# An adaptive-LayerNorm transformer block: gates applied to the results instead of folded into the weights, queries masked by VectorE instead of placed by DMA, blocks in plain order

## The chip, the cores and the metric

The kernel runs on one core of one Trainium2 chip. The metric is the time of one execution on the device in microseconds (us), the median of several runs. A core has five engines that run their own instruction queues in order: TensorE (PE, matrix products into PSUM), VectorE (DVE), ScalarE (ACT), GpSimd (POOL) and SyncE (SP, which here only issues DMAs).

## The reference

Input `x` is 2048 rows of 512 columns, bf16; attention has 32 heads of 16 columns. A conditioning row `c` gives shifts, scales and gates.

```python
mod = (_silu(c) @ w_mod).reshape(c.shape[0], 6, 1, -1)
sa, ca, ga, sb, cb, gb = ...                       # six rows of 512
h = _layernorm(x, axis=-1) * (1 + ca) + sa
x = x + ga * _A_ref(h, A_wqkv, A_wo)               # attention, then @ wo
h = _layernorm(x, axis=-1) * (1 + cb) + sb
x = x + gb * _B_ref(h, B_w1, B_b1, B_w2, B_b2)     # @ w1 + b1, gelu, @ w2 + b2; 1376 hidden columns

# _A_ref
scores = jnp.einsum('bhqd,bhkd->bhqk', q, k) * Dh ** (-0.5)
p = _softmax(scores, axis=-1)
o = jnp.einsum('bhqk,bhkd->bhqd', p, v)
```

32 heads with 2048 x 2048 scores each are 134 million exponentials. They are the largest piece of work in the kernel.

## The kernel before

The program is written by a scheduler inside the kernel: every piece of work is an `op` with an engine, a guessed duration and its dependencies, and the order in which each engine's queue stands is decided while the program is built. On the chip the queues are fixed.

Attention goes in 32 runs. A run takes one block of 512 queries and four heads of one group of eight (`cc` is the group, 0 to 3), against 16 key tiles of 128 keys. For each key tile there are four score matmuls of 128 x 512, one per head. The exponentials of a key tile go one of two ways:

```python
# ACT: two or three score tiles at a time, PSUM -> bf16
nc.scalar.activation(out=e.tile[:, 0:len(got) * QB], in_=o.tile[:, 0:len(got) * QB],
                     func=ACT.Exp, scale=ESC)                                     # L842, pt<-st
# DVE: an exponential out of integer arithmetic: the score as bits of a bf16 ...
nc.vector.tensor_scalar(out=ph.tile[:, ...], in0=o.tile, scalar1=PH_B, scalar2=0.0,
                        op0=ALU.add, op1=ALU.max)                                 # L883, ph<-ax, 4 per key tile
# ... and four shifted copies, whose weighted sum smooths the error
nc.vector.tensor_scalar(out=o.tile, in0=first.tile, scalar1=PH_SH[j], scalar2=None,
                        op0=ALU.add)                                              # L898, sh<-ph, 4 per key tile
```

Four of the 16 key tiles of a run (`DKS = (2, 6, 10, 14)`; one of 16 in the first run) may go to DVE. When ACT has nothing else to do it takes one of these too; the scheduler decides which. Either way the products with the values gather in the PSUM bank `od` (L931). So ACT and DVE share the exponentials, and PE feeds both.

The parts that the change touches:

```python
# queries: one scaled evacuation, then eight DMAs into a tile that is zero elsewhere
# (two tiles side by side, the even and the odd heads)
qs = op("DVE", lambda o: nc.vector.tensor_scalar(
    out=o.tile, in0=mm.tile[:, 0:QB], scalar1=QSC, scalar2=None, op0=ALU.mult), ...)   # L695
def place(o):
    for i in range(8):
        at = slice(16 * i, 16 * i + 16)
        nc.sync.dma_start(out=qm.tile[at, i % 2, :], in_=qs.tile[at, :])               # L702

# order of runs: two blocks of queries with the first group of heads, then the two with the second
early = [(1, 0),(0, 1),(1, 1)]
groups = [(0, 0)] + early + [(b, cc) for b in range(NQ) for cc in range(NC) if ...]

# gates: GpSimd multiplies the weights once, in halves of 256 columns
def scaled(parts, gate_t, deps):
    for w in parts:
        got += beside(lambda c, w=w: nc.gpsimd.tensor_tensor(
            out=w()[:, c], in0=w()[:, c], in1=gate_t[:, c], op=ALU.mult), deps, prio=2.0)
...
# so a residual is one add that reads the product from PSUM, for each 128 rows
nc.vector.tensor_tensor(out=x2.tile[:, t, :], in0=a.tile, in1=xr.tile[:, t, :], op=ALU.add)   # L1137
nc.vector.tensor_tensor(out=o.tile, in0=mm.tile, in1=x2.tile[:, t, :], op=ALU.add)            # L1185
```

The last block of 512 queries is taken in two halves. The first half's projection and MLP are done while the second half's attention runs; of its 11 slices of hidden columns the first `PSUM_F = 4` are evacuated by DVE into `g` (L1164) and get their gelu after the last exponential, and the other seven are multiplied after it and go through gelu straight from PSUM (L1160). Gelu and exponential use different tables of ACT, so gelus of the last block are put after the last exponential. The tail after it then holds the second half's projection, residual, LayerNorm and MLP (L1220 to L1281).

Of the kernel before, what the change touches and what calls it, by code (L numbers as in the profile page):

```python
# [12 lines left out]
ALU = mybir.AluOpType  # L13
# [238 lines left out]
def kernel(  # L252
# [14 lines left out]
    nc = tc.nc  # L267
# [23 lines left out]
    AHEAD = 3  # L291
    PSUM_F = 4
    FIRST_DKS, D_TIME = (14,), 8.0
# [10 lines left out]
    def res(name, n, shape, dt, pool=work):  # L304
        return Res(name, n, lambda i: pool.tile(shape, dt, name=f"{name}{i}"))
# [15 lines left out]
                                   work.tile([P, TPB], FP32, name=f"rs{i}")))  # L321
    QM = [keep.tile([P, 2, QB], BF16, name=f"qm{n}") for n in range(4)]
    r_qm = Res("qm", 4, lambda i: QM[i])
    r_qs = res("qs", 2, [P, QB], BF16)
    r_OD = res("OD", 2, [P, QB], FP32)
    r_RB = res("RB", 1, [P, QB], FP32)
    r_OT = res("OT", 6, [P, QB], BF16)
    r_OS = res("OS", 2, [P, QB], BF16)
    r_o = res("o", 2, [P, D], BF16)
    r_dc = res("dc", 2, [P, 16], FP32)  # L330
# [79 lines left out]
    def dma(fn, deps=(), kb=64, eng="SP", n=1, **k):  # L410
        o = op(eng, fn, 0.45 * n, deps, **k)
        o.kb = kb
        return o
# [270 lines left out]

    o_qz = [op("POOL", lambda o, n=n: nc.gpsimd.memset(QM[n], 0.0), 1.0, prio=0.5 + n) for n in range(1, 4)]

    def make_q(b, cc, kind, acq):
        qm = op("NIL", None, 0.0, (), lat=0.0, prio=0.0, acq=r_qm)
        mm = proj(b, o_w[0], cc, kind, acq, after=qm)
        if (b, cc) == (0, 0):  # L690
            evs = [op("DVE", lambda o, p=p: nc.vector.tensor_scalar(
                out=qm.tile[:, p, :], in0=mm.tile[:, 0:QB], scalar1=qmask[:, p:p + 1], scalar2=None,
                op0=ALU.mult), 0.6, (mm, qm, o_mask), prio=0.1 if p == 0 else 0.45, rel=(mm,)) for p in range(2)]
        else:
            qs = op("DVE", lambda o: nc.vector.tensor_scalar(  # L695
                out=o.tile, in0=mm.tile[:, 0:QB], scalar1=QSC, scalar2=None, op0=ALU.mult), 0.6, (mm, qm),
                prio=0.3, acq=r_qs, rel=(mm,))

            def place(o):
                for i in range(8):  # L700
                    at = slice(16 * i, 16 * i + 16)
                    nc.sync.dma_start(out=qm.tile[at, i % 2, :], in_=qs.tile[at, :])  # L702
            evs = 2 * [dma(place, [qs] + o_qz, kb=128, n=8, prio=0.4, rel=(qs,))]
        o_q[(cc, b)] = (qm, evs)
        qm.uses += 1
        q_left[(cc, b)] = 8 * NT
# [30 lines left out]

    early = [(1, 0),(0, 1),(1, 1)]
    groups = [(0, 0)] + early + [(b, cc) for b in range(NQ) for cc in range(NC) if (b, cc) not in [(0, 0)] + early]
    runs = [(b, 2 * cc + p) for b, cc in groups[:LAST * NC] for p in range(2)] + [(LAST, u) for u in range(8)]  # L740
    wait = {cc: 2 * groups.index((0, cc)) for cc in range(NC)}
    NR = len(runs)
# [259 lines left out]

    def scaled(parts, gate_t, deps):
        got = []
        for w in parts:
            got += beside(lambda c, w=w: nc.gpsimd.tensor_tensor(
                out=w()[:, c], in0=w()[:, c], in1=gate_t[:, c], op=ALU.mult), deps, prio=2.0)
        return op("NIL", None, 0.0, got, lat=0.0, prio=0.0)

    def w2_scaled():  # L1010
        return scaled([lambda f=f: W2[f // 4].tile[:, f % 4, :] if f < 8 else W2c[:, f - 8, :] for f in range(NF)],
                      gb_bc, (W2[0], W2[1], o_late["small"], o_late["gb"]))

    def beside(fn, deps, rel=(), prio=0.5):
# [68 lines left out]


    def wo_mm(ps, b, t, lo, hi):
        for u in range(lo, hi):
            ot, at = (o_OT[(b, (t // 2) * NC + u)], (t % 2) * P) if b == LAST else (o_OT[(b, u)], t * P)
            nc.tensor.matmul(out=ps, lhsT=ot.tile[:, at:at + P], rhs=Wo[:, u, :],
                             start=(u == 0), stop=(u == NC - 1))
# [34 lines left out]
    def block_tail(b, nt=TPB):  # L1124
# [8 lines left out]
        for t in range(nt):  # L1133
            a = chain([(lambda ps, t=t, u=u: wo_mm(ps, b, t, u, u + 1), MM) for u in range(NC)],
                      [x for u in ots for x in u.two] + [prev], kind, r_ax, ots, 2)
            prev = a
            res_done.append(op("DVE", lambda o, t=t, a=a: nc.vector.tensor_tensor(  # L1137
                out=x2.tile[:, t, :], in0=a.tile, in1=xr.tile[:, t, :], op=ALU.add), 0.6,
                (a, xr), prio=0.1, rel=(a,)))
        h, hd, za, trs = layer_norm(lambda t: x2.tile[:, t, :], res_done, modB, o_late["mB"],  # L1140
# [39 lines left out]
        for t in range(nt):  # L1180
            mm = chain([(lambda ps, t=t, f=f: w2_mm(ps, g.tile, t * P, f, f + 1), MM)
                        for f in range(NF)], (prev, one, o_late["w2"]), "part" if part else kind, r_ax, (g,), 3,
                       lambda f: ge[0] if not part else ge[f >= 2] if f < PSUM_F else ev[f])
            prev = mm
            a = op("DVE", lambda o, t=t, mm=mm: nc.vector.tensor_tensor(  # L1185
                out=o.tile, in0=mm.tile, in1=x2.tile[:, t, :], op=ALU.add), 0.6,
                (mm,), prio=3.0 if part else 0.1, acq=r_o, rel=(mm, x2))
            dma(lambda o, t=t, a=a: nc.sync.dma_start(
                out=out[0][b * QB + t * P:b * QB + (t + 1) * P, :], in_=a.tile), (a,), kb=128,
                rel=(a,))  # L1190
# [3 lines left out]
    def last_half():  # L1194
# [17 lines left out]
        for n, t in enumerate(tiles):  # L1212
# [18 lines left out]
            def wo2(o, t=t):  # L1231
                for p in range(2):
# [4 lines left out]
                   ml + [early[t]], lat=PEL, mode=full, kind="last", prio=0.2)  # L1237
            a = op("DVE", lambda o, t=t: nc.vector.tensor_tensor(
                out=x2.tile[:, t, :], in0=acc[t].tile, in1=xr.tile[:, t, :], op=ALU.add), 0.62,
                (w, x2, xr), prio=0.024 + n / 50, rel=(acc[t],))  # L1240
            s = op("DVE", lambda o, t=t: stats(ln, t, x2.tile[:, t, :]), 0.83, (a, ln), prio=0.022 + n / 50)
# [31 lines left out]
            for f in range(NF):  # L1273
# [6 lines left out]
                prev = o  # L1280
            a = op("DVE", lambda o, t=t, first=first: nc.vector.tensor_tensor(  # L1281
                out=o.tile, in0=first.tile, in1=x2.tile[:, t, :], op=ALU.add), 0.66, (prev,), prio=0.1,
                acq=r_o, rel=(first,))
            dma(lambda o, t=t, a=a: nc.sync.dma_start(
# [6 lines left out]
    for b in range(NQ):  # L1291
# [14 lines left out]
        make_v(b, 0, kind, r_ax, "DVE")  # L1306
    o_w[0].uses += 1
    for cc in range(1, NC):
        due(32 + APR * (2 * cc - 1) - CB + (wait[cc] - 2 * cc) * APR * 1, CB * 0.7 / 8 + 0)
        for b in range(NQ):  # L1310
            make_k(b, cc, f"c{cc}", r_ax, "DVE", o_k[(0, min(b + AHEAD, LAST))])
            make_v(b, cc, f"c{cc}", r_ax, "DVE", o_k[(0, min(b + AHEAD, LAST))])
# [9 lines left out]
    def want_q(g):  # L1322
        while q_made[0] < g and q_made[0] + 1 < NQ * NC:
            q_made[0] += 1
            b, cc = groups[q_made[0]]
            due(32 + APR * (first_run(q_made[0]) - 1) - 32)
            make_q(b, cc, f"q{q_made[0]}", r_ax)
            due(1e9)
            if cc == NC - 1:
                o_h[b].uses -= 1  # L1330

    state = {"late": 0}
    qk_a()
    want_q(1)
    while True:
# [7 lines left out]
        while ended:  # L1343
# [4 lines left out]
            for cc in range(1, NC):  # L1348
                if r >= wait[cc] - 3:
                    urgent.add(f"c{cc}")  # L1350
                if r >= 2 * cc - 3:
                    urgent.add(f"in{cc}")
# [4 lines left out]
            if r == 0:  # L1357
                late_loads(o_last[0])
                o_late["ga"] = gate_bc(ga_bc, o_late[2], "gate")
                o_late["wo"] = scaled([lambda u=u: Wo[:, u, :] for u in range(NC)] +  # L1360
                                      [lambda p=p: WoP[:, p, :] for p in range(2)], ga_bc,
                                      (o_late["wo"], o_late["ga"]))
                lt = {3: o_late[3], 4: o_late[4]}
                gt = o_late["g"]

                class V:
                    pass
                va, vb = V(), V()
                o_late["mB"] = None
                state["gt"] = gt  # L1370
# [9 lines left out]
            if r == 6:  # L1380
                for i in range(2):
                    W2[i] = load_w(B_w2[4 * i * P:4 * (i + 1) * P, :].rearrange(
                        "(j p) n -> p j n", p=P), r_w, (), prio=5.0)
                o_late["w2"] = w2_scaled()
                state["w2"] = True
# [38 lines left out]
```

## Time and profile before

| what | value |
|---|---|
| time, median of 3 runs | 797.8 us (797.3 to 799.59) |
| span of the profiled execution | 795.5 us |
| granted TensorE clock, mean | 0.996 |
| exponentials on ACT (L842), 631 instructions | 717.5 us busy |
| `ph` and `sh` on DVE (L883, L898), 472 each | 308.2 and 309.7 us busy |
| residual adds from PSUM (L1137, L1185, L1238, L1281), 32 | 0.68 to 0.69 us each |
| weight multiplications on GpSimd (L1006), 34 | 0.67 to 0.68 us each |
| `qm<-qs` DMAs, 120 of 16 KB | issue 0.58 us each (median) on SP |
| first exponential starts | 16.0 us |
| last exponential ends | 770.6 us |

A line of the groups names the source line, the engine, the operation and `out<-in` by the program's names, with shapes and count; after the bar stand the busy time of the group and the mean nanoseconds of one instruction, then the idle time of the engine just before it and what ended most of that. A line of the waits says who waited for whom: microseconds in total, times, the longest. The chain that ended last goes back from the last instruction to what released it, step by step, and gives the shares of the span by engine.

### The profile page before, as it was taken

Reading aid. Unit: us, or ns where it says so; the run is one execution under the profiler, and the core shown is the slowest. Engines: PE = TensorE matmul, PEld = TensorE weight load, DVE = VectorE, ACT = ScalarE, POOL = GpSimd, SP = SyncE. Lnnn points to the kernel's source line nnn. Section 1 sums busy time; section 2 is a strip of 40 time slices with the busy share of each in tenths; the row PEclk is TensorE's granted clock in tenths of the full one; section 3 lists DMA queues with packets and bytes.
Section 4 is the critical chain, followed back from the end, with each engine's and each line's share of the span. In section 5 each row is a group of like instructions: output and inputs, shape, how many; then the busy total and the mean of one; then the engine's idle time right before and its main releaser. Section 6 shows DMA issues by size and latency. Waiting matters only on the chain.

```text
span 795.5 us, 20495 instructions
## 1 busy us (share of the span) xinstructions
PE 728.9 (92%) x8240; PEld 274.1 (34%) x8322; DVE 735.8 (92%) x1276; ACT 760.3 (96%) x689; POOL 124.2 (16%) x274
## 2 busy tenths in 40 slices
PE   8889999899999998898999999999999899999998
PEld 3333333333333322223222232322234343343455
DVE  6779799999999999999999989999999999999993
ACT  3899999999999999999999999999999999999994
POOL 5610304022124410110000200000000100000100
PEclk9999999999999999999999999999999999999999
DMA  6025001010012010000100000000110001100010
GB/s 212 28 67 153 24 24 43 13 28 9 20 23 72 20 47 23 19 16 20 35 19 22 26 15 29 19 23 19 35 54 21 22 19 35 29 16 25 24 45 27
DMA packets 37521, 28.22 MB, mean 35 GB/s; under 512 B 16405, under 2 KB 32822, under 8 KB 37426
## 3 DMA queue, kind: packets, MB, share of 16 engines
q1 hardware_dynamic: 36362, 25.86, 11.4%
q8 instruction: 65, 1.06, 0.5%
q10 hardware_dynamic: 1064, 1.05, 0.4%
q14 instruction: 30, 0.25, 0.1%
HBM read 21.30 MB, written 2.61 MB: 30 GB/s over the span
## 4 chain that ended last, share of the span: by engine, by line
ACT 31%; PE 30%; DVE 25%; issue 10%; DMA 2%; SPq 1%; POOL 0%; DVEq 0%; ACTq 0%
ACT pt L842 29%; PE od L931 10%; DVE sh L898 9%; DVE ph L883 9%; PE st L793 8%; PE ax L1094 3%; PE ax L793 2%; PE ax L1154 2%; DMA dc<-dn 2%; DVE OD L956 1%; DVE ln_s L580 1%; PE ax L674 1%; DVE g L1164 1%; ACT g L1173 1%; PE ax L711 1%
## 5 line engine op out<-in xcount | busy, mean ns | idle before, releaser
L842 ACT ACTIVATE pt<-st 128x1536 bf16<-128x1536 f32 (+1 forms) x631 | 717.5, 1294 | 8.8 <-PE ax L793 4.4
L883 DVE TENSOR_SCALAR ph<-ax 128x512 int16<-128x512 f32 x472 | 308.2, 681 | 22.5 <-PE ax L793 20.7
L898 DVE TENSOR_SCALAR sh<-ph 128x2048 int16<-128x2048 int16 x472 | 309.7, 695 | 0.8 <-PE od L931 0.4
L793 PE MATMUL st<-qm,kT 32*128 32x512 bf16 x1576 | 247.3, 383 | 30.5 <-ACT pt L842 25.5
L931 PE MATMUL od<-sh,VX 128*32 128x512 bf16 (+1 forms) x2384 | 167.6, 341 | 7.0 <-DVE sh L898 5.9
L793 PE MATMUL ax<-qm,kT 32*128 32x512 bf16 x472 | 163.3, 380 | 7.4 <-DVE ph L883 4.2
L793 PEld LDWEIGHTS <-kT 32*128 32x128 bf16 x2048 | 79.4, 91 | 239.5 <-issue 229.0
L931 PE MATMUL od<-pt,VEB 128*32 128x512 bf16 (+1 forms) x1964 | 147.1, 341 | 1.0 <-issue 0.5
L931 PEld LDWEIGHTS <-VEB 128*32 128x32 bf16 x2560 | 64.2, 96 | 77.6 <-issue 63.1
L931 PEld LDWEIGHTS <-VX 128*32 128x32 bf16 x2384 | 59.9, 95 | 88.9 <-issue 79.5
L983 POOL TENSOR_TENSOR OT<-OD,RB 128x256 bf16<-128x256 f32 x38 | 27.9, 745 | 316.8 <-DVE sh L898 203.3
L931 PE MATMUL od<-ph,VEB 128*32 128x512 bf16 (+1 forms) x596 | 46.8, 339 | 2.3 <-DVE OD L956 2.2
L983 POOL TENSOR_TENSOR OS<-OD,RB 128x256 bf16<-128x256 f32 x24 | 17.7, 751 | 137.6 <-DVE sh L898 85.6
L1154 PE MATMUL ax<-blk,W 128*128 128x512 bf16 (+1 forms) x126 | 36.2, 369 | 1.7 <-issue 0.8
L727 POOL TENSOR_SCALAR VX<-VEB 128x128 bf16<-128x128 bf16 x64 | 23.5, 367 | 74.9 <-DVE VEB L606 71.2
L674 PE MATMUL ax<-blk,w 128*128 128x512 bf16 x93 | 30.8, 390 | 3.9 <-issue 1.5
L1094 PE MATMUL ax<-w,g 128*128 128x512 bf16 x101 | 28.9, 383 | 1.7 <-DVE xb L1137 0.8
L1164 DVE TENSOR_SCALAR g<-ax,b1c 128x512 bf16<-128x512 f32 (+1 forms) x37 | 26.3, 714 | 0.4 <-PE ax L1154 0.3
L1094 PEld LDWEIGHTS <-g 128*128 128x128 bf16 x176 | 14.5, 98 | 25.3 <-issue 14.8
L580 DVE BATCH_NORM_STATS2 ln_s<-xb 128x6 f32<-128x512 bf16 x32 | 21.5, 673 | 0.6 <-DMA xb<-in_A_x_dram 0.5
L956 DVE COPY OD<-od 128x512 f32<-128x512 f32 x31 | 21.1, 680 | 0.7 <-issue 0.4
L1154 PEld LDWEIGHTS <-W 128*128 128x128 bf16 x176 | 14.1, 97 | 20.4 <-issue 14.1
(111 smaller groups left out, 377.5 us busy)
## 6 DMA issues: line engine op xcount, KB each, us to landing
RB<-rn SPq DMA_DIRECT2D x124, 64.0 KB
xb<-in_A_x_dram SPq DMA_DIRECT2D x8, 512.0 KB
out_dram<-o SPq DMA_DIRECT2D x16, 128.0 KB
qm<-qs SPq DMA_DIRECT2D x120, 16.0 KB
w<-in_A_wqkv_dram SPq DMA_DIRECT2D x3, 512.0 KB
W<-in_B_w_dram SPq DMA_DIRECT2D x1, 1376.0 KB
blk<-in_w_mod_dram ACTq DMA_DIRECT2D x2, 512.0 KB
g<-in_w_mod_dram SPq DMA_DIRECT2D x2, 512.0 KB
```

The source lines that it names most:

```text
L580: nc.vector.bn_stats(out=st6, in_=src)
L674: return chain([(lambda ps, j=j: nc.tensor.matmul(out=ps[:, 0:QB], lhsT=w.tile[:, j, cc * P:(cc + 1) * P], rhs=o_h[b].tile[:, j, :], start ...
L793: nc.tensor.matmul(out=o.tile[:, k * QB:(k + 1) * QB], lhsT=kT[cc][kb][rows, ko * P:(ko + 1) * P], rhs=qm.tile[rows, par, :] if hb is None ...
L842: nc.scalar.activation(out=e.tile[:, 0:len(got) * QB], in_=o.tile[:, 0:len(got) * QB], func=ACT.Exp, scale=ESC)
L883: nc.vector.tensor_scalar(out=ph.tile[:, o.row * QB:(o.row + 1) * QB], in0=o.tile, scalar1=PH_B, scalar2=0.0, op0=ALU.add, op1=ALU.max)
L898: sh = op("DVE", lambda o, j=j: nc.vector.tensor_scalar(out=o.tile, in0=first.tile, scalar1=PH_SH[j], scalar2=None, op0=ALU.add), 0.6, es, ...
L931: nc.tensor.matmul(out=o_od[r].tile[32 * i:32 * i + 32, n * HB:n * HB + w], lhsT=v_tile(kt, ph)[:, c0:c0 + 32], rhs=got[i][:, at:at + w], ...
L956: OD = op("DVE", lambda o: nc.vector.tensor_copy(out=o.tile, in_=od.tile), 0.6, (last,), prio=0.0, acq=r_OD, rel=(od,))
L983: two = beside(lambda c: nc.gpsimd.tensor_tensor(out=OT.tile[:, c], in0=OD.tile[:, c], in1=o5.tile[:, c], op=ALU.mult), (OT,), (OD, o5))
L1094: nc.tensor.matmul(out=ps, lhsT=g[:, f, col:col + P], rhs=rhs, start=(f == 0), stop=(f == NF - 1))
L1154: mm = chain([(lambda ps, f=f, j=j: nc.tensor.matmul(out=ps[:, 0:N], lhsT=W1[:, j, f * P:(f + 1) * P], rhs=h.tile[:, j, 0:N], start=(j == ...
L1164: ev.append(op("DVE", lambda o, f=f, mm=mm: nc.vector.tensor_scalar(out=g.tile[:, f, 0:N], in0=mm.tile[:, 0:N], scalar1=b1c[:, f:f + 1], s ...
```

## The change

The change has four parts. The gates `ga` and `gb` are no longer multiplied into the weights: each residual becomes a multiplication by the gate that reads PSUM and an add in SBUF, both on DVE, and GpSimd's 34 multiplications leave. The queries are evacuated by one DVE instruction that writes both masked copies, and the DMAs and the zeroed tiles leave. The runs stand in plain order: all heads of block 0, then block 1, and so on. And `PSUM_F` is 8 instead of 4. The purpose of the version with these four is a simpler data flow: nothing waits for scaled weights or for placed queries, a block's projection and MLP can begin as soon as its own eight runs are done, and less of the MLP is left for the tail.

```diff
-    PSUM_F = 4
+    PSUM_F = 8
...
-            qs = op("DVE", lambda o: nc.vector.tensor_scalar(
-                out=o.tile, in0=mm.tile[:, 0:QB], scalar1=QSC, scalar2=None, op0=ALU.mult), 0.6, (mm, qm),
-                prio=0.3, acq=r_qs, rel=(mm,))
-
-            def place(o):
-                for i in range(8):
-                    at = slice(16 * i, 16 * i + 16)
-                    nc.sync.dma_start(out=qm.tile[at, i % 2, :], in_=qs.tile[at, :])
-            evs = 2 * [dma(place, [qs] + o_qz, kb=128, n=8, prio=0.4, rel=(qs,))]
+            evs = 2 * [op("DVE", lambda o: nc.vector.tensor_tensor(
+                out=qm.tile, in0=mm.tile[:, 0:QB].unsqueeze(1).to_broadcast([P, 2, QB]),
+                in1=qmask.unsqueeze(2).to_broadcast([P, 2, QB]), op=ALU.mult), 1.14, (mm, qm, o_mask),
+                prio=0.3, rel=(mm,))]
...
-    early = [(1, 0),(0, 1),(1, 1)]
-    groups = [(0, 0)] + early + [(b, cc) for b in range(NQ) for cc in range(NC) if (b, cc) not in [(0, 0)] + early]
-    runs = [(b, 2 * cc + p) for b, cc in groups[:LAST * NC] for p in range(2)] + [(LAST, u) for u in range(8)]
-    wait = {cc: 2 * groups.index((0, cc)) for cc in range(NC)}
+    runs = [(b, u) for b in range(NQ) for u in range(8)]
...
-    def scaled(parts, gate_t, deps):        # and w2_scaled, and their calls
...
     # block_tail, after the projection (and alike in the tail of the last half)
-            res_done.append(op("DVE", lambda o, t=t, a=a: nc.vector.tensor_tensor(
-                out=x2.tile[:, t, :], in0=a.tile, in1=xr.tile[:, t, :], op=ALU.add), 0.6,
-                (a, xr), prio=0.1, rel=(a,)))
+            y = op("NIL", None, 0.0, (a, x2, o_late["ga"]), lat=0.0, prio=0.0, acq=r_y)
+            m = op("DVE", lambda o, t=t, a=a, y=y: nc.vector.tensor_tensor(
+                out=y.tile, in0=a.tile, in1=ga_bc, op=ALU.mult), 0.6, (y,), prio=0.1, rel=(a,))
+            res_done.append(op("DVE", lambda o, t=t, y=y: nc.vector.tensor_tensor(
+                out=x2.tile[:, t, :], in0=y.tile, in1=xr.tile[:, t, :], op=ALU.add), 0.33,
+                (m, xr), prio=1.5, rel=(y,), port=True))
...
     # after the second layer, the same with gb_bc and the output tile
-            a = op("DVE", lambda o, t=t, mm=mm: nc.vector.tensor_tensor(
-                out=o.tile, in0=mm.tile, in1=x2.tile[:, t, :], op=ALU.add), 0.6,
-                (mm,), prio=3.0 if part else 0.1, acq=r_o, rel=(mm, x2))
+            m = op("DVE", lambda o, mm=mm, y=y: nc.vector.tensor_tensor(
+                out=y.tile, in0=mm.tile, in1=gb_bc, op=ALU.mult), 0.6, (y,), prio=3.0 if part else 0.1,
+                rel=(mm,))
+            a = op("DVE", lambda o, t=t, y=y: nc.vector.tensor_tensor(
+                out=o.tile, in0=y.tile, in1=x2.tile[:, t, :], op=ALU.add), 0.33,
+                (m, o_late["gb"]), prio=3.0 if part else 1.5, acq=r_o, rel=(y, x2), port=True)
...
-        due(32 + APR * (2 * cc - 1) - CB + (wait[cc] - 2 * cc) * APR * 1, CB * 0.7 / 8 + 0)
+        due(32 + APR * (2 * cc - 1) - CB, CB * 0.7 / 8)      # when keys and values of group cc are due
```

The durations in these calls (0.6, 0.33, 1.14) are the scheduler's guesses.

## The prediction

> **What bounds the kernel now.** I read the page's busy shares and the chain of work that ended last, then the groups by form for what one instruction costs, then busy time by stage, then the waits.
>
> ```profile
> PE 728.9 (92%) x8240; PEld 274.1 (34%) x8322; DVE 735.8 (92%) x1276; ACT 760.3 (96%) x689; POOL 124.2 (16%) x274
> ...
> ACT 31%; PE 30%; DVE 25%; issue 10%; DMA 2%; SPq 1%; POOL 0%; DVEq 0%; ACTq 0%
> ```
>
> ScalarE (ACT) is fullest, yet the chain goes in near equal parts over three engines: they run in lockstep, each mostly just in time for the next. So I ask where each has slack:
>
> ```profile
> core 0: us, PE busy (x) PEld busy (x) DVE busy (x) ACT busy (x) POOL busy (x), PEclk, DMA share, GB/s
> 0.00:20.00 20.00, 16.18 (x125) 7.61 (x126) 13.44 (x31) 7.77 (x10) 10.90 (x48) 1.00 0.68 211
> 20.00:100.00 80.00, 69.71 (x720) 28.70 (x727) 63.62 (x122) 76.66 (x72) 23.64 (x81) 1.00 0.23 67
> 100.00:760.00 660.00, 612.16 (x7024) 218.26 (x7093) 637.34 (x1083) 652.60 (x564) 86.70 (x140) 0.99 0.10 26
> 760.00:795.50 35.50, 30.87 (x378) 19.53 (x380) 21.36 (x43) 23.30 (x47) 3.01 (x6) 1.00 0.12 36
> ```
>
> From 100 to 760 us ACT is idle 660 - 652.6 = 7.4 us (1.1%): it is the bound. VectorE (DVE) is idle 22.7 us there (3.4%) and 16.4 us between 20 and 100: little, but not nothing. The waits inside 120 to 755 us say what DVE's idle time is, and ACT's:
>
> ```profile
> DVE ph L883 <- PE ax L793: 12.1, 21, 1.7
> DVE dc L967 <- DMA dc<-dn: 5.0, 7, 1.9
> ...
> ACT pt L842 <- PE ax L793: 3.9, 8, 1.3
> ACT pt L842 <- PE st L793: 1.8, 5, 0.6
> ```
>
> DVE's idle time is waiting for scores, in few pieces; ACT hardly waits at all. What one instruction costs:
>
> ```profile
> L842 ACT ACTIVATE pt<-st 128x1536 bf16<-128x1536 f32 x315 | 474.8, 1507 | 5.7 <-PE ax L793 2.4 <-PE st L793 2.3 <-PE od L931 0.3
> L842 ACT ACTIVATE pt<-st 128x1024 bf16<-128x1024 f32 x315 | 341.2, 1083 | 3.1 <-PE ax L793 2.0 <-PE st L793 0.8
> L898 DVE TENSOR_SCALAR sh<-ph 128x2048 int16<-128x2048 int16 x472 | 309.7, 695 | 0.8 <-PE od L931 0.4
> L883 DVE TENSOR_SCALAR ph<-ax 128x512 int16<-128x512 f32 x472 | 308.2, 681 | 22.5 <-PE ax L793 20.7 <-PE st L793 0.4
> L695 DVE TENSOR_SCALAR qs<-ax 128x512 bf16<-128x512 f32 x15 | 10.2, 681 | 0.7 <-PE ax L674 0.3 <-PE st L793 0.2
> L1185 DVE TENSOR_TENSOR o<-ax,xb 128x512 bf16<-128x512 f32 x14 | 9.5, 680 | 1.7 <-PE ax L1094 1.7
> ```
>
> Recorded times overlap. In the timeline eight shifts (`sh<-ph`) in a row from 765.55 us take 4.89 us, 0.61 each and not 0.695, so I take 0.605 us as the pitch of a DVE instruction recorded at 0.68 and subtract 0.075 from the others. Summed over all of before's DVE instructions these pitches give 725 us, against 735.8 measured.
>
> [...] 44 of the 472 shifts last over 720 ns, up to 1223, together 7.6 us above the usual 683 ns, each with a GpSimd operation beside or just before it.
>
> **The change part by part**, counted from the two programs.
>
> Gates. The 32 adds that read PSUM (14+14+2+2) become 32 multiplications by the gate that read PSUM, at the same price, and 32 more adds in SBUF. [...] In exchange GpSimd loses 34 weight multiplications of 0.675 us (23 us). It is 16% busy, so that alone is worth nothing, but some 15 of the 44 lengthened shifts stand beside such a multiplication: about 2 us of DVE come back.
>
> Queries. 15 evacuations of 512 columns (0.605) become 15 of 1024 columns with a mask[...]. 120 DMAs of 16 KB and three memsets leave. PE waited for these DMAs about 2 us in all, so removing them is worth little.
>
> The threshold PSUM_F, 4 to 8. In the last half block four more of the eleven hidden slices go over DVE during attention: 4 x (0.471 - 0.075) = 1.6 us of DVE. After attention, 16 matmuls of 256 columns (28 take 3.4 us in before's tail, 0.12 each: 2.0 us) and four gelu instructions of 0.468 us leave; one gelu of two slices becomes one of six, about 1.48 instead of 0.62 us (slope from 512 columns in 0.624 us and 5632 in 4.897).
>
> Split of the exponentials. The scheduler reacts with one key tile: 468 instead of 472 instructions each of `ph` and `sh` on DVE, which saves 8 x 0.605 = 4.8 us; ACT gets one more 1536 and one more 1024 instruction and loses one of 512: 1.507 + 1.083 - 0.591 = 2.0 us, less an overlap of 0.16 (816.0 us of recorded exponentials fill 717.5 us in 631 instructions): +1.8 us.
>
> DVE sum: 11.2 + 8.2 + 1.6 - 4.8 = +16.2 us[...].
>
> Order of runs. Block 0 is now finished first. Keys and values of the second group of heads are needed at run 2, not at run 4, so these evacuations move forward, into the stage where DVE has 16.4 us idle. Added up along the program, the changed DVE queue is 5 us ahead in work by run 5 (about 167 us in before), 14 by the last run. So about 5 us fall where they cost nothing, about 9 into the stage with 22.7 us of slack.
>
> The sum on the path. (a) ACT +1.8 us: the bound itself, comes through whole. (b) 9 us less 2 of DVE in the steady stage raise it from 96.6 to about 97.6% beside an ACT at 99%; an engine that full makes its neighbours wait now and then. I let 40% of 7 us come through, +2.8 us; this share is a judgement. (c) The tail, from the last exponential at 770.6 us: PE has 2 us less, and the second-layer products of the first two tiles now stand ahead of the last tiles' work instead of behind it. But the multiplications add a third of a microsecond at each of three places on the chain (two residuals, the output), and these products delay the third tile's transposes by about 2 us. Step by step I get 0.4 us less: -0.5. Total 797.8 + 1.8 + 2.8 - 0.5 = 801.9, predicted 802.
>
> **Rivals.** DVE becomes the bound: all 16 us come through, less the tail, about 813. For it: DVE's share of the chain is 25%, and several 20 us stretches are 19.9 to 20.0 us busy. Against it: 39 us of idle time between 20 and 760 us, and a scheduler that moved only one tile. All hidden: the DVE work fills the waits for scores, and the DMA waits (`dc<-dn`, 5 us) shrink as 120 DMAs leave the same queue: 797.8 + 1.8 - 0.5, about 799, or 797 if the tail gives 2 us. The early stage starves: K and V of the second group now have to be projected while the first runs need PE, and ACT, idle only 3.3 us between 20 and 100, waits some 3 to 5 us more: about 806. For it: the chain of the first 120 us is 38% ACT, and run 2 begins at 74.7 us where run 4 began at 122.0; against it: PE has 10 of 80 us free and DVE 16.
>
> **Range and chances.** All hidden with a good tail, 797, to early starvation together with the 40% share, 808: the range is 797 to 809. The 2% border above is 813.8, which needs DVE as the bound: 6%. 2% faster would need ACT to lose 16 us, and nothing takes work from it: 2%.
>
> **What would show it.** Right: DVE busy about 750 us, ACT about 761; the new SBUF add recorded near 0.42 us and `qm` near 1.22; DVE's wait for scores shorter than 20.7 us; from the last exponential to the end 24 to 25 us. Wrong: ACT idle in the steady stage well above 7.4 + 3 us with DVE or PE's wait for `sh` as releaser (then DVE is the bound); ACT idle before 100 us above 3.3 + 2 us (starvation); [...] or a tail off by more than 1.5 us.

## The result, and the profile after

| | kernel before | changed kernel |
|---|---|---|
| time, median of 4 runs | 798.69 us (797.3 to 799.59) | 792.48 us (790.91 to 793.12) |
| ratio | 1 | 0.9921, 95% interval 0.9897 to 0.9945 |
| span of the profiled execution | 795.5 us | 791.0 us |
| ACT idle from first to last exponential | 10.7 us | 5.3 us |
| exponentials on ACT, time covered | 717.5 us | 718.4 us |
| last exponential ends | 770.6 us | 766.2 us |
| from there to the end of the last output DMA's issue | 22.4 us | 22.3 us |

The changed kernel is 0.8% faster. 802 us was predicted, with a range from 797 to 809, so the prediction missed, and in its direction too. (Ratios leave disturbed runs out, so one can differ slightly from the quotient of the medians beside it.)

The page of the changed kernel, busy shares and the shares of the chain that ended last:

```profile
PE 732.0 (93%) x8185; PEld 273.2 (35%) x8266; DVE 744.1 (94%) x1304; ACT 760.2 (96%) x686; POOL 97.1 (12%) x237
...
ACT 39%; PE 24%; DVE 20%; issue 13%; DMA 2%; POOL 0%; SPq 0%; POOLq 0%; DVEq 0%; ACTq 0%
```

DVE has 8.3 us more to do, ACT as much as before, and yet the end comes 4.5 us sooner. The chain has moved to ACT, 39% for 31%: the other two engines hold it up less. Busy time by stage of the changed kernel, cut at the same places of the work:

```profile
20.00:100.00 80.00, 74.18 (x768) 31.41 (x778) 66.62 (x126) 76.86 (x72) 29.98 (x95) 1.00 0.22 66
100.00:755.00 655.00, 610.97 (x6950) 216.89 (x7013) 643.53 (x1101) 652.79 (x566) 56.00 (x93) 1.00 0.08 23
755.00:791.00 36.00, 30.43 (x354) 17.31 (x354) 21.89 (x48) 23.07 (x42) 3.01 (x6) 0.99 0.13 39
```

The gain lies in the steady stage: ACT is idle 655 - 652.8 = 2.2 us where it was idle 7.4, and DVE 11.5 where it was 22.7. The stage from 20 to 100 us has 3.1 us of idle ACT, where it had 3.3; it did not starve. The waits of the changed kernel between 120 and 755 us (who waited for whom: us in total, times, longest):

```profile
PE od L920 <- DVE sh L887: 4.1, 17, 0.4
DVE ph L872 <- PE ax L782: 3.9, 10, 1.4
...
ACT pt L831 <- PE st L782: 1.1, 2, 0.9
DVE dc L956 <- DMA dc<-dn: 0.9, 2, 0.5
```

DVE's wait for the normalisation's DMA went from 5.0 us to 0.9, its wait for scores from 12.1 to 3.9, ACT's for scores of the `ax` kind from 3.9 to 0.2. What one instruction costs, by form (busy us, mean ns, then idle time before it):

```profile
L831 ACT ACTIVATE pt<-st 128x1536 bf16<-128x1536 f32 x316 | 478.9, 1515 | 2.1 <-PE st L782 1.2 <-PE od L920 0.3 <-PE ax L782 0.2
...
L872 DVE TENSOR_SCALAR ph<-ax 128x512 int16<-128x512 f32 x468 | 305.6, 680 | 14.1 <-PE ax L782 12.6
L692 DVE TENSOR_TENSOR qm<-ax,qmask 128x1024 bf16<-128x1024 f32 x15 | 18.2, 1213 | 0.1
L1120 DVE TENSOR_TENSOR y<-ax,ga_bc 128x512 bf16<-128x512 f32 x14 | 9.5, 681 | 0.2 <-PE ax L1070 0.2
L1122 DVE TENSOR_TENSOR xb<-y,xb 128x512 bf16<-128x512 bf16 x14 | 6.0, 427 | 0.0
```

The prices were near what was looked for: 427 ns for the add in SBUF (near 0.42 us), 1213 for the masked queries (near 1.22), 681 for the multiplication (680 for the old add). The 11.2 and 8.2 us of DVE in the prediction's sum were estimates of mine that no run had shown by then. With 75 ns taken off as there, the 32 recorded adds (424 to 427 ns) make 11.2 us, and 15 x (1213 - 75 - 605) ns make 8.0. So the sum of instructions was sound; what failed is what it was taken to do to the waits.

### The profile page after: what moved, and what is told of

Same layout as the page of the kernel before. It is cut to its first block, busy times and chain, and to the rows that moved or that the text cites. A ratio compares the mean times of both kernels' runs of the same rounds, so it can differ in the third digit from the quotient of the medians.

```text
span 791.0 us, 20209 instructions
## 1 busy us (share of the span) xinstructions
PE 732.0 (93%) x8185; PEld 273.2 (35%) x8266; DVE 744.1 (94%) x1304; ACT 760.2 (96%) x686; POOL 97.1 (12%) x237
## 4 chain that ended last, share of the span: by engine, by line
ACT 39%; PE 24%; DVE 20%; issue 13%; DMA 2%; POOL 0%; SPq 0%; POOLq 0%; DVEq 0%; ACTq 0%
ACT pt L831 38%; PE od L920 8%; DVE ph L872 7%; PE st L782 7%; DVE sh L887 6%; PE ax L1076 3%; PE ax L782 2%; DVE g L1149 1%; DVE qm L692 1%; PE ax L1139 1%; DVE ln_s L579 1%; PE ax L673 1%; DMA dc<-dn 1%; DMA xb<-in_A_x_dram 1%; DVE z L590 1%
## 5 line engine op out<-in xcount | busy, mean ns | idle before, releaser
L831 ACT ACTIVATE pt<-st 128x1536 bf16<-128x1536 f32 x632 | 718.4, 1304 | 3.0 <-PE st L782 2.1
L887 DVE TENSOR_SCALAR sh<-ph 128x2048 int16<-128x2048 int16 x468 | 303.2, 687 | 1.4 <-PE od L920 0.9
L782 PEld LDWEIGHTS <-kT 32*128 32x128 bf16 x2048 | 82.8, 91 | 243.4 <-issue 233.4
L920 PEld LDWEIGHTS <-VEB 128*32 128x32 bf16 x2560 | 62.6, 96 | 79.0 <-issue 66.5
L920 PEld LDWEIGHTS <-VX 128*32 128x32 bf16 x2352 | 58.3, 95 | 83.3 <-issue 71.8
L1139 PE MATMUL ax<-blk,W 128*128 128x512 bf16 (+1 forms) x144 | 39.0, 358 | 1.5 <-issue 0.5
L1149 DVE TENSOR_SCALAR g<-ax,b1c 128x512 bf16<-128x512 f32 (+1 forms) x41 | 28.2, 691 | 0.2
L1076 PEld LDWEIGHTS <-g 128*128 128x128 bf16 x176 | 13.9, 97 | 21.9 <-issue 11.2
```

The lines of the kernel that those rows point to most:

```text
L782: nc.tensor.matmul(out=o.tile[:, k * QB:(k + 1) * QB], lhsT=kT[cc][kb][rows, ko * P:(ko + 1) * P], rhs=qm.tile[rows, par, :] if hb is None ...
L887: sh = op("DVE", lambda o, j=j: nc.vector.tensor_scalar(out=o.tile, in0=first.tile, scalar1=PH_SH[j], scalar2=None, op0=ALU.add), 0.6, es, ...
L920: nc.tensor.matmul(out=o_od[r].tile[32 * i:32 * i + 32, n * HB:n * HB + w], lhsT=v_tile(kt, ph)[:, c0:c0 + 32], rhs=got[i][:, at:at + w], ...
L1076: nc.tensor.matmul(out=ps, lhsT=g[:, f, col:col + P], rhs=rhs, start=(f == 0), stop=(f == NF - 1))
L1139: mm = chain([(lambda ps, f=f, j=j: nc.tensor.matmul(out=ps[:, 0:N], lhsT=W1[:, j, f * P:(f + 1) * P], rhs=h.tile[:, j, 0:N], start=(j == ...
L1149: ev.append(op("DVE", lambda o, f=f, mm=mm: nc.vector.tensor_scalar(out=g.tile[:, f, 0:N], in0=mm.tile[:, 0:N], scalar1=b1c[:, f:f + 1], s ...
```

## Experiments

Eighteen kernels ran. "The kernel before" was run beside each, with medians from 797.5 to 799.5 us. The changed kernel was written once more with its four parts as switches; the order of every queue with all four off or all four on is that of the two kernels. Line numbers differ from kernel to kernel. The expectations name theories by letters; each says what it means.

A time of one kernel also goes with the clock that TensorE was granted in that execution: of the kernel before beside `r_before_gpsimd_queue`, the quickest run took 794.7 us at a mean clock of 1.0, the longest 806.43 us at 0.981. Where I give a "time at full clock", it is the intercept of a straight line through all runs of that kernel, time over the mean granted clock of each run.

### One part alone on the kernel before

The four switches, one at a time: `FLAG_Q` (queries masked by DVE), `FLAG_O` (plain order), `FLAG_P` (`PSUM_F = 8`), `FLAG_G` (gates on DVE).

```diff
-FLAG_G, FLAG_Q, FLAG_O, FLAG_P = 0, 0, 0, 0
+FLAG_G, FLAG_Q, FLAG_O, FLAG_P = 0, 1, 0, 0      # and so on, one each
```

With gates on DVE and placed queries together, there is one `qs` buffer instead of two; this holds for every run with both.

Queries masked: 

> The kernel before with one part of the change: queries masked by one DVE instruction (1.21 us each, 15 of them) instead of evacuated and placed by 120 DMAs. The program gives ACT 8 score tiles of 512 more (1584 instead of 1576) and DVE 8 ph and 8 sh fewer. Theory A (the query DMAs and what they hold up on SP's queue cost the kernel before its idle time on ACT): faster by 3 to 5 us, DVE's wait for dc from 5.0 us to under 2. Theory B (the order of the runs is the gain): same or up to 3 us slower, because ACT has 3.6 us more to do. Theory C (the gain is how this particular static order happens to fall): anything within 3 us either way, without a pattern among the four single parts.

Plain order: 

> The kernel before with plain order of runs alone. ACT gets 1584 score tiles, DVE 8 ph and 8 sh fewer. Theory B (block tails begin 4 runs earlier, with more room between them, and key and value work moves into the early idle time of DVE): faster by 3 to 5 us. Theory A: same or up to 3 us slower, with DVE's wait for dc staying near 5 us. Theory C: within 3 us either way.

`PSUM_F`: 

> The kernel before with PSUM_F 8 alone. Same 1576 score tiles on ACT. My working of the tail says 16 matmuls (2.0 us of PE) and four gelus leave the tail: tail from last exponential to the end shorter by 1 to 2 us, 1.6 us of DVE more before it: time between 0 and 2 us lower. Theories A and B expect no more than that; theory C within 3 us either way.

Gates: 

> The kernel before with gates multiplied on DVE alone (and one buffer instead of two for the evacuated queries, for room). 1580 score tiles on ACT, DVE 11.2 us of adds more, 34 GpSimd multiplications fewer. [...] Theories A and B: slower by 1 to 5 us. Theory C: within 3 us either way.

### One part undone on the changed kernel

```diff
-FLAG_G, FLAG_Q, FLAG_O, FLAG_P = 1, 1, 1, 1
+FLAG_G, FLAG_Q, FLAG_O, FLAG_P = 1, 0, 1, 1      # and so on, one each
```

Gates folded into the weights again: 

> The changed kernel with one part undone: gates folded into the weights by GpSimd again. The single parts were not additive (order alone and gates alone each cost about 10 us, all four together save 6). Theory I (order and gates need each other: folded weights stand in the way of early block tails, and gates on DVE need the room that plain order gives): about as slow as order alone, 800 to 808 us. Theory C (each plan falls by luck within some microseconds): 790 to 800, without relation. ACT has 1588 score tiles, 8 more than the changed kernel (+3.6 us), which both theories include.

The order with two blocks first again: 

> The changed kernel with the order of runs undone (blocks 0 and 1 in turns). ACT has 1588 score tiles, 8 more. Theory I: as slow as gates alone, 803 to 810 us, with a granted clock near 0.98. Theory C: 790 to 800.

Queries placed by DMA again: 

> The changed kernel with the queries placed by DMA again (one buffer for the evacuated queries). 1584 score tiles, 4 more (+1.8 us). Query alone gave 1.0 us at full clock. Theory A, as far as it is left: 793 to 796 us, with DVE's wait for dc back at 3 to 5 us. Theory I: the same, since the queries are outside its pair. Theory C: 790 to 800.

`PSUM_F = 4` again: 

> The changed kernel with PSUM_F 4 again. 1580 score tiles, as in the changed kernel. PSUM_F alone gave nothing that could be told from zero; all theories but C expect 791 to 795 us, theory C 788 to 798.

Measured, all eight. "Tiles" are the score tiles of 512 columns that the plan gives ACT (2048 less four for each key tile on DVE); the last three columns are from the profiled execution: exponentials and idle time of ACT between first and last exponential, and DVE's wait at the reciprocal.

| run | median us | ratio, 95% interval | tiles | exponentials us | ACT idle us | dc wait us |
|---|---|---|---|---|---|---|
| kernel before | 797.5 and 798.9 | 1 | 1576 | 717.5 | 10.7 | 5.6 |
| + masked queries | 797.46 | 0.9989, 0.9968 to 1.0011 | 1584 | 720.3 | 9.1 | 0.3 |
| + plain order | 808.10 | 1.0131, 1.0095 to 1.0167 | 1584 | 722.6 | 17.6 | 7.4 |
| + `PSUM_F = 8` | 797.70 | 1.0002, 0.9977 to 1.0026 | 1576 | 717.5 | 8.5 | 4.7 |
| + gates on DVE | 809.83 | 1.0148, 1.0109 to 1.0188 | 1580 | 720.4 | 17.2 | 5.2 |
| changed kernel | 792.48 | 0.9921, 0.9897 to 0.9945 | 1580 | 718.4 | 5.3 | 0.9 |
| - gates on DVE | 798.95 | 1.0005, 0.9983 to 1.0028 | 1588 | 721.9 | 7.3 | 0.4 |
| - plain order | 796.19 | 0.9968, 0.9952 to 0.9985 | 1588 | 720.7 | 6.0 | 1.0 |
| - masked queries | 808.28 | 1.0104, 1.0069 to 1.0139 | 1584 | 722.0 | 17.4 | 8.5 |
| - `PSUM_F = 8` | 792.41 | 0.9919, 0.9890 to 0.9948 | 1580 | 718.0 | 5.5 | 0.8 |

`PSUM_F` does nothing either way. The other three are not additive at all. With placed queries, plain order costs 10 us, gates on DVE cost 12, and both (with `PSUM_F`) 10. With masked queries neither costs anything (0.9968 and 1.0005, each with `PSUM_F`), and both together gain 6. Masked queries alone gain nothing: ACT's idle time falls by 1.6 us and its exponentials cover 2.8 more. So the masked queries, which I had valued at 8.2 us of DVE against next to nothing, are what the other two parts need; with their DMAs back, the changed kernel loses 16 us. None of the theories foresaw this: plain order alone, gates alone and queries placed again came out slower than every range set for them, and masked queries alone missed theory A's 3 to 5 us.

What the DMAs did is seen in the kernel before, in its timeline from 607 to 617 us (start, duration, instruction; in brackets the idle time before it and who ended it):

```profile
607.02 0.67 DVE L956 COPY OD<-od 128x512 f32<-128x512 f32 x1
...
607.72 0.53 SPq L962 DMA_DIRECT2D dn<-OD  x1
...
608.92 5.98 SPq L702 DMA_DIRECT2D qm<-qs  x8
...
614.96 0.57 SPq L964 DMA_DIRECT2D dc<-dn  x1
616.79 0.25 DVE L967 RECIPROCAL dc<-dc 128x16 f32<-128x16 f32 x1 [1.90 <-DMA dc<-dn]
```

A run of attention ends with a normalisation: the sums go out by DMA (`dn<-OD`), come back across the partitions (`dc<-dn`), and DVE takes their reciprocal. SyncE's queue is in order: eight query DMAs, here 5.98 us of issues, stand between the two, so `dc<-dn` is issued 7.24 us after `dn<-OD`; the median of the 31 normalisations is 1.72. DVE's queue is in order too: it stands 1.90 us at the reciprocal. Counting the normalisations with four or more query DMAs issued between the copy of the sums (`OD<-od`) and `dc<-dn`: 7 of 31 in the kernel before, 7 and 8 with plain order or gates added, 6 in the changed kernel with placed queries, none in any kernel with masked ones. The queue fits the pattern, but these runs don't prove it: with placed queries, scores also have to wait for the DMAs themselves (PE 0.4 us and its weight loads 0.7 in the changed kernel with placed queries), and each switch lets the scheduler move other work. Nor does it account for all of it. TensorE's clock is cut to half now and then, for 3.41 us or a multiple (the last section tells of it); of these spells between 20 and 765 us, 1 of 5 with plain order alone and 1 of 4 with gates alone begin within 5 us after a wait at the reciprocal.

### The queue alone

First, idle DMAs that the scheduler knows of:

```diff
+            i1 = dma(idle, evs[:1], kb=128, n=8, prio=0.4, acq=r_idle)   # eight copies of 8 KB of zeros
+            free(i1, (i1,))                                              # into a tile that nobody reads
```

> The changed kernel with its masked queries kept, and after each query eight idle DMAs of 8 KB on SyncE's queue, which nothing waits for: the queue is as full of issues as with placed queries, but no score waits for it. Theory A (the query DMAs stand ahead of the normalisation's DMAs in SyncE's queue, so DVE stands at its reciprocal, PE pauses and the clock is halved for a spell): DVE's wait dc<-dn comes back to 4 us or more, clock below 0.992, 798 to 806 us. Theory B (it is the way of the query through the DMAs, which delays the scores): 791 to 794 us, dc waits under 2 us.

Measured: 802.27 us, ratio 1.0029 (1.0007 to 1.0051), dc wait 2.0 us, mean clock 0.9925. Ten us slower than the changed kernel, as theory A says, but with less of a wait and a higher clock than it said, and not for its reason alone: the scheduler, seeing SyncE fuller, gave ACT three instructions more, and the exponentials took 722.3 us instead of 718.4. So the same DMAs once more, issued where the scheduler does not see them:

```diff
+            def mask(o):
+                nc.vector.tensor_tensor(out=qm.tile, ...)             # the masked queries, as they were
+                for i in range(8):
+                    nc.sync.dma_start(out=idle[16 * i:16 * i + 16, :], in_=x_idle[16 * i:16 * i + 16, :])
```

> The changed kernel with all five queues in the order they had, and only SyncE's with eight idle DMAs of 8 KB more at each query (120 in all), which the scheduler doesn't know of. Theory A (the queue's load delays the normalisation's DMAs and so DVE, PE and the clock): DVE's wait dc<-dn 4 us or more, clock below 0.994, 796 to 803 us. Theory D (the cost of idle DMAs, 10 us in the run before, came from the plan that the scheduler made around them, which gave ACT more score tiles): 791.5 to 794.5 us, dc wait under 2 us.

Measured: 807.87 us (800.79 to 810.7), ratio 1.0126 (1.0080 to 1.0171), mean clock of the runs 0.983. Every other queue has the order of the changed kernel (GpSimd clears one tile more at the start), the data are the same, nothing waits for the idle DMAs, and the time is that of the kernel with placed queries. Theory D is out. Theory A has the direction; the cost is 5 us above its range. The profile was taken of the quickest of its runs; its waits from 120 to 755 us, and the worst place in the timeline:

```profile
PE od L948 <- DVE sh L915: 7.8, 17, 2.8
DVE dc L984 <- DMA dc<-dn: 7.7, 5, 3.2
```

```profile
519.36 0.53 SPq L979 DMA_DIRECT2D dn<-OD  x1
...
520.70 4.94 SPq L709 DMA_DIRECT2D idle<-x_idle  x8
525.69 0.58 SPq L981 DMA_DIRECT2D dc<-dn  x1
527.61 0.25 DVE L984 RECIPROCAL dc<-dc 128x16 f32<-128x16 f32 x1 [3.21 <-DMA dc<-dn]
527.78 1.22 DVE L915 TENSOR_SCALAR sh<-ph 128x2048 int16<-128x2048 int16 x2
528.46 0.40 PE L948 MATMUL od<-sh,VX 128*32 128x512 bf16 x4 [2.85 <-DVE sh L915]
...
529.76 1.45 ACT L859 ACTIVATE pt<-st 128x1536 bf16<-128x1536 f32 x1 [2.95 <-PE st L810]
```

This is the whole chain: 4.94 us of issues, DVE 3.21 us at the reciprocal, PE 2.85 us for the shift behind it, ACT 2.95 us for scores behind that. It is the issue of `dc<-dn` that is late: in the three waits of over 1 us the reciprocal starts 1.8 to 1.9 us after that issue, and in the changed kernel's two waits 2.9 and 3.5 us after it. And it is not over then. The same place by stretches (PE, PEld, DVE, ACT, POOL busy, then the granted clock):

```profile
515.00:525.00 10.00, 9.97 (x108) 3.24 (x105) 9.18 (x15) 10.00 (x10) 0.00 (x0) 1.00 0.06 18
525.00:529.00 4.00, 1.15 (x19) 0.31 (x11) 1.39 (x4) 1.81 (x2) 0.00 (x0) 0.99 0.07 10
529.00:535.00 6.00, 6.00 (x56) 1.54 (x52) 5.26 (x10) 4.26 (x4) 0.00 (x0) 0.72 0.14 46
```

From 525 to 529 us no engine does as much as half its time. Then, from 528.91, the clock is granted at half for 3.41 us (0.72 over the stretch): PE is busy all of the 6 us, and ACT idle 1.7 of them, of which 0.76 still belong to the wait above. Here a wait is paid for a second time in the clock.

### The wait taken away, and the DMAs moved to another queue

The reciprocal planned 2 us later in DVE's queue, so that other work stands ahead of it:

```diff
-        o3 = op("DVE", lambda o: nc.vector.reciprocal(out=o2.tile, in_=o2.tile), 0.2, (o2,),
+        o3 = op("DVE", lambda o: nc.vector.reciprocal(out=o2.tile, in_=o2.tile), 0.2,
+                (op("NIL", None, 0.0, (o2,), lat=2.0, prio=0.0),),
```

On the kernel before: 

> The kernel before with the same one edit: the reciprocal planned 2 us later. Theory A, which has 5.6 us of DVE's wait for the reciprocal's DMA as the first part of the gain: wait under 1.5 us, 794 to 796 us. Theory B and the theory that plans merely scatter: 797 to 799 us or anything from 793 to 803.

Measured: 796.12 us, ratio 0.9938 (0.9912 to 0.9964); the dc wait is gone; theory A's range is missed by a hair. By the ratio this edit brings most of what the whole change brings, by the medians about half (796.1 us beside 799.5, where the changed kernel had 792.2 in the same batch), though ACT got three exponentials more (720.4 us). It does not isolate the wait: the order of DVE's queue changed far and wide.

On the changed kernel with placed queries: 

> The changed kernel with placed queries (808.3 us before this edit, DVE's wait dc<-dn 8.5 us), but with the reciprocal planned 2 us later in DVE's queue, so that DVE no longer stands waiting for its DMA. Theory A: dc waits under 2 us, clock back above 0.991, 796 to 801 us. Theory B: dc waits gone too, but the time stays at 804 to 809 us, with PE's waits for qm<-qs unchanged.

Measured: 811.57 us, ratio 1.0137 (1.0104 to 1.0170): a miss. The wait is gone and the last exponential ends at 775.4 us instead of 781.9, but here too the edit changed the order of DVE's queue far and wide, and the time from the last exponential to the end grew from 22.2 us to 28.2. Most of this is a late start: GpSimd's last scaling of attention results (`OT<-OD`) begins 1.7 us after the last exponential, where without the edit it begins 2.6 us before it. The run tells nothing for either theory.

The query DMAs issued by GpSimd, with every order as it was:

```diff
-                    nc.sync.dma_start(out=qm.tile[at, i % 2, :], in_=qs.tile[at, :])
+                    nc.gpsimd.dma_start(out=qm.tile[at, i % 2, :], in_=qs.tile[at, :])
```

On the changed kernel with placed queries: 

> The changed kernel with placed queries (808.3 us, DVE's wait dc<-dn 8.5 us), every queue in the same order, but the query DMAs issued by GpSimd instead of SyncE. Theory A (SyncE's queue): dc wait under 3 us, 795 to 802 us. Theory B (scores wait for the queries' way through DMAs): 805 us or more, waits for qm<-qs unchanged or longer, since GpSimd issues them after its multiplications.

Measured: 804.42 us, ratio 1.0061 (1.0038 to 1.0085), dc wait from 8.5 us to none, time at full clock from 799.3 to 795.0. That is between the two expectations: 3.9 us, where theory A said 6 or more. The profile shows where part of the rest is; GpSimd works in order as well (timeline from 634.5 to 640 us, the lines in question):

```profile
634.24 1.92 POOL L713 DMA_DIRECT2D qm<-qs  x4
...
636.50 0.72 POOL L593 TENSOR_TENSOR rs<-rs,mhalf 128x2 f32<-128x2 f32 x1
637.25 0.73 DVE L597 TENSOR_SCALAR z<-xb,mv,rs 128x512 bf16<-128x512 bf16 x2 [1.60 <-POOL rs L593]
...
638.64 0.38 PE L659 MATMUL ax<-ident,z 128*128 128x128 bf16 x4 [1.93 <-DVE ph L894]
```

Now a LayerNorm stands behind the query DMAs, DVE waits 1.60 us for it, PE 1.93 us for DVE, and at 639.82 the clock goes to half for 13.65 us. The block moved from one queue to another. PE waits 0.4 us for `qm<-qs` in the kernel with placed queries and its weight loads 0.7, neither waits here; this speaks against theory B.

On the kernel before: 

> The kernel before with the same move of its query DMAs to GpSimd's queue. Theory A: dc wait from 5.6 us to under 2, 793 to 797 us. Theory B[...]: 798 us or more.

Measured: 797.36 us, ratio 0.9979 (0.9952 to 1.0007), dc wait from 5.6 us to 1.4, but lengthened shifts of DVE from 44 (7.6 us in excess) to 54 (10.1). No difference that these runs can show, and theory A's range is just missed. So with the order of every queue held, taking most of the wait from the kernel before is not shown to gain anything; the longer shifts may hide a gain.

### How much a plan is luck

> The changed kernel with one constant of the scheduler that none of the theories speaks of (how far ahead ACT's choice looks: 0.12 instead of 0.15 us), so that the order of the queues falls out differently and nothing else changes. Theories A and B: within 2 us of the changed kernel, 790.5 to 794.5. Theory C (the order of the queues scatters by several us whatever the change, and the four parts only drew a lucky one): 795 us or more, with some 5 us more of idle ACT.

Measured: 792.16 us, ratio 0.9919 (0.9895 to 0.9943). The constant turned out to move nothing: every queue of ACT and DVE has the order it had. It is a repetition of the changed kernel, and no test of theory C. But its profiled execution (796.8 us, clock 0.989) has 9.1 us of idle ACT where the changed kernel's has 5.3: with the same order of queues, the idle time of one profile moves by some 4 us. A constant that does move the queues, on both kernels:

```diff
-    SLACK = {"NIL": 0.0, "PE": 0.10, "DVE": 0.05, "ACT": 0.15, "POOL": 0.05, "SP": 0.05}
+    SLACK = {"NIL": 0.0, "PE": 0.10, "DVE": 0.06, "ACT": 0.15, "POOL": 0.05, "SP": 0.05}
```

Before: 

> The kernel before with one constant of the scheduler changed (how far apart two candidates for DVE may start and still be ranked by priority: 0.06 instead of 0.05 us): another order of the queues, two to four score tiles more on ACT. Theory C (plans scatter by several us, the kernels stand where their constants were tuned): 800 to 806 us. If the kernel before is no lucky plan: 797 to 800 us.

After: 

> The changed kernel with the same edit. Theory C: 796 to 802 us, so that the gap between the two kernels is within what plans scatter. If the gain belongs to the data flow: 791 to 795 us, still 5 us or more ahead of the kernel before with this edit.

Measured: before 812.18 us, ratio 1.0167 (1.0127 to 1.0208); after 796.62 us, ratio 0.9972 (0.9953 to 0.9992). Both lose, in this one step of one constant. But the kernel before loses 14 us and the changed one 4, and the gap between them grows to 15.6 us. The kernel before is above both its ranges; the changed kernel is in theory C's range (796 to 802), but the gap is the 5 us or more that the other theory asked for. The first list is that of the kernel before with the edit, the second that of the changed kernel with it (120 to 755 us), where no wait for `dc<-dn` is left:

```profile
DVE ph L894 <- PE ax L804: 17.7, 28, 1.6
DVE dc L978 <- DMA dc<-dn: 6.6, 7, 1.6
```

```profile
DVE ph L894 <- PE ax L804: 6.4, 16, 1.4
```

In the edited kernel before, 9 normalisations have query DMAs ahead of `dc<-dn`, counted as above, instead of 7. Over all plans, the six kernels with masked queries and no idle DMAs lie between 792.4 and 799.0 us; of the nine with query DMAs in SyncE's queue, three lie between 796.1 and 798.7 and six at 807.6 or more. I take it that a plan with placed queries is good only where these blocks happen to fall well, and that the order with two blocks first and the gates folded into the weights are a setting in which they did; this is argued, not shown.

### More zero matmuls

The scheduler adds zero matmuls where PE would be idle, meant to keep the clock up (by the last section's counts, half clock followed 2 of 3119 stretches with PE busy 90% or more, and 13 of 16 below 60%). More of them in the kernel before:

```diff
-HEAT = 1.3
+HEAT = 1.5
```

> The kernel before with more zero matmuls (the scheduler adds them where PE was busy less than 1.5 instead of 1.3 us in the last 3.4 us). If half-clock spells are a cause of their own: mean clock 0.996 or more, and the time 2 us below that of the kernel before with the slack edit, which moves as many score tiles. If they are only a sign of waits with other causes: clock and time as with that edit, or slower for the matmuls added.

Measured: 807.63 us, ratio 1.0114 (1.0077 to 1.0151), mean clock 0.9935, against 0.984 and 812.18 us of the kernel before with the slack edit; the kernel before itself has 0.991 to 0.993. ACT is idle 17.3 us and DVE waits 6.3 us for `dc<-dn`. Beside the kernel before the clock is hardly better, and the time is 9 us worse. Neither expectation is met. The edit is no clean test, as it moved the queues too; that filler alone would cure the waits is not borne out.

## Why the prediction was wrong

Its sum was (a) +1.8 for the exponentials moved to ACT, (b) +2.8 for a fuller DVE, (c) -0.5 for the tail, on 797.8 us. Between the profiled executions, from one end to the other: first exponential +0.2, exponentials +0.9, other work of ACT -0.2, ACT idle -5.4, tail -0.1, together -4.6 us, which but for rounding is the difference of the spans. (The medians differ by 6.2; the runs of the changed kernel also had the higher clock, 0.9965 on average, where those of the kernel before have 0.991 to 0.993 in the batches of the experiments, at some 0.5 us per 0.001.)

**(b) failed, and in sign.** The step said "an engine that full makes its neighbours wait now and then. I let 40% of 7 us come through, +2.8 us; this share is a judgement." ACT's idle time did not rise by 2.8 us, it fell by 5.4. DVE's load went up and its idle time down: its wait at the reciprocal fell by 4.1 us, its wait for scores by 8.2. The judgement treated waiting as a function of how full an engine is; in `d_idle_same` the same work in the same order waits more, ACT 12.9 us instead of 5.3 in its quickest run, only because a DMA queue is fuller. How much of the 5.4 us came this way stays open. In the profile of the kernel before, ACT's pauses of over 0.15 us after 100 us sum to 6.4 us; 2.2 of them end within 6 us after a wait at the reciprocal, and 1.7 follow the cut of the clock at 280.54 us, which no such wait precedes. In the changed kernel they sum to 1.6; but, as `d_other_plan` showed, one profile's idle time moves by some 4 us.

**The step ahead of it, in the part on queries, is where the answer was missed:** "PE waited for these DMAs about 2 us in all, so removing them is worth little." True of the DMAs' own consumers, and even of the kernel before as it stands (masked queries alone: ratio 0.9989), but not with the other parts. `d_idle_same` shows that in the changed kernel DMAs which have no consumer cost 15 us when they stand in that queue. Who waits behind an instruction in the same queue had to be asked as well. The line for it was in the prediction's own fence (`DVE dc L967 <- DMA dc<-dn: 5.0, 7, 1.9`), and the rival "all hidden" named it ("the DMA waits (`dc<-dn`, 5 us) shrink as 120 DMAs leave the same queue"), but counted no gain for it. It was the nearest of the rivals.

**(a) had the right mechanism and half the size:** one key tile went to ACT, as counted from the queues, and the exponentials cover 0.9 us more instead of 1.8. The recorded times of the two forms sum to 823.9 us where they summed to 816.0, and cover 718.4 where they covered 717.5: they overlap by more than the 0.16 us that I took off.

**(c) was about right:** -0.1 for -0.5, 24.8 us to the end of the span where 24 to 25 was said. Some of this may be luck: the shorter tail was credited to `PSUM_F`, which alone left the tail at 25.1 us, where it was 24.9. ACT's part of the tail begins with the load of the gelu's table, 1.28 us in both profiles.

**The counts of DVE** were near in price and somewhat high in sum: 744.1 us busy instead of 750. The shifts gave back more than the 2 us set for them: those over 720 ns went from 44 to 21, their excess from 7.6 to 3.4 us, 4.2 us. Each of the 44 and of the 21 overlaps a GpSimd instruction in time; of the other shifts, 15 of 428 do in the kernel before and 16 of 447 in the changed kernel. What makes a shift longer beside GpSimd was not shown.

**The rivals.** DVE as the bound: out, DVE is idle 28.0 us between first and last exponential. Early starvation: out, 3.1 us of idle ACT from 20 to 100 us, 3.3 before.

What each part is worth has no single answer, as the table shows. With queries masked, gates and order still matter, by 6.5 and 3.7 us, and in the profiles somewhat over half of it through the split: without either, the scheduler gives ACT two key tiles more, and the exponentials cover 721.9 or 720.7 us instead of 718.4. Why it does so was not tried. How much of the changed kernel's 4 us lead over its own slack edit is a matter of tuned constants stays open too.

## What to carry to other kernels

When DMAs are removed from or added to a queue, look at what stands behind them in it, not only at who waits for their data: in the changed kernel 120 small DMAs that nobody waited for cost 15 us, because a chain of short DMAs that DVE needs had to be issued in between. A short wait of an in-order engine for a DMA can deserve more weight than its length, as at 527.61 us above, where DVE stood 3.21 us, and PE and ACT then nearly as long (2.85 and 2.95 us). And before a part is valued alone, remember that the schedule around it was tuned with the other parts in place; a small neutral edit on both versions gives a first hint which one is the sturdier.

## What the runs showed of the hardware

A pause of PE can be followed by slow matmuls: at 280.54 us of the kernel before, after 3.41 us in which PE was busy for 2.46, the clock goes to half for 3.41 us, and the score matmuls (`st<-qm,kT`) in it take 604 ns (median), where the 22 in the 10 us from 270 take 384. Every cut of the clock that begins between 20 and 765 us in these traces is to one half and lasts 3.41 us or a multiple (6.83, 10.24, 13.65). The two in the kernel before begin at 280.54 and 563.85 us, 83 times 3.41 us apart but for rounding. I cut the traces with such a cut in the stretch from 20 to 765 us into stretches of 3.41 us in step with it. Of 3119 stretches at full clock in which PE was busy 90% or more, 2 were followed by half clock; of 1107 between 70 and 90%, 25; of 34 between 60 and 70%, 8; of 16 below 60%, 13. So PE need not be idle for a whole stretch: 8 of those with PE busy between 60 and 70% were followed by half clock. By what rule the clock is cut was not shown.

What this costs: within the runs of one kernel, time falls on a line with the mean granted clock, by 0.33 to 0.63 us for each 0.001, mostly near 0.5 (one kernel with four runs aside). The idle DMAs lowered it from 0.9965 to 0.983, which at 0.45 to 0.6 us is an estimated 6 to 8 of their 15 us; the rest I put down to the waits themselves (6.8 us more at the reciprocal in the profiled run). The line does not tell the slow matmuls from the pauses that led to them. One spell of 3.41 us lowers the mean by 3.41 x 0.5 / 795 = 0.0021, about 1 us by this line, again an estimate. So a kernel near its bound can pay for a wait first as the wait, and then again in the clock, as `d_idle_same` does from 525 us on.
